# A transformer block with segment memory: the feed-forward part moved into the planned order, and work of the attention and opening stages placed on other engines

## The chip, the cores and the metric

The kernel runs on one core of one Trainium2 chip. A core has five engines that run side by side, each with its own queue in a fixed order: TensorE (PE in the profile) multiplies matrices, VectorE (DVE), ScalarE (ACT) and GpSimd (POOL) work on elements, SyncE (SP) issues DMAs. PSUM is the memory into which PE writes, in eight banks of 128 x 512 fp32; SBUF holds everything else on the chip. The metric is the time of one execution on the device in microseconds, lower is better. The time is the median of several runs.

## The reference, cut to what matters

```python
mod = (silu(c) @ w_mod)                  # six vectors of 512: sa, ca, ga, sb, cb, gb
h = layernorm(x) * (1 + ca) + sa         # x: 2048 x 512
q, k, v = h @ wq, h @ wk, h @ wv         # 32 heads of 16; 4 segments of 512 tokens
for s in range(4):                       # M, z: each head's memory, zero at first
    p = softmax(q_s k_s^T / 4 + causal mask)
    a_mem = phi(q_s) M / (phi(q_s) z + 1e-6)       # phi(t) = t + 1 if t > 0 else exp(t)
    o_s = g * a_mem + (1 - g) * p v_s              # g = sigmoid(beta), one per head
    M, z = M + phi(k_s)^T v_s, z + sum phi(k_s)
x = x + ga * (o @ wo)
h = layernorm(x) * (1 + cb) + sb
x = x + gb * (relu(h @ w1 + b1)**2 @ w2 + b2)      # 512 -> 1792 -> 512
```

All tensors are fp32.

## The kernel before, in words

**Precision.** A projection's two operands are each split into a high part, rounded to fp32r by a cast on ACT, and a low part, the rest, by a subtraction (`tensor_tensor`). Each product is three matmuls: high by high, high by low, low by high.

**Order.** The opening and the attention are written as nodes with `op(engine, duration, function, priority, after, get, put)`. `Plan.run` (L136) plays them through on a model with estimated durations: each engine takes the ready node of the lowest priority whose buffers are free, PE with some reluctance (`STAY`, `BATCH`, `PATIENCE`) to change between its three ways of tiling the array: R (row tiles), C (column tiles), F (full). `PL.emit()` then writes the instructions of PE, DVE, ACT and POOL in that order, which is fixed; waits keep it correct. SP's order comes from the framework. `POOLS` says how many buffers there are: eight PSUM banks, of which groups #A, #B, #V, #D may hold 4, 3, 1, 3 at a time, and SBUF buffers by name. The constants `K_...` are due times, in half units of attention.

**Opening.** DMAs bring x of the first segment, two parts of w_mod, then wq, wk, wv. `consts` loads c and beta on ACT's queue. `mod_cols` makes the shift and scale (`modc`). `ln1` normalises four tiles of 128 tokens, `ln_transposed` (L430) turns each on PE, applies scale and shift (two pieces of 128 columns on ACT, two on DVE, into one of two `oraw` buffers) and splits it into HT. `split_w` (L458) splits a weight in four row pieces: casts on ACT, subtractions on DVE and POOL in turn. Fourteen matmuls on the identity (L319) run ahead. `clear` fills rows of ST with zeros.

**Attention.** A unit u is 8 heads of one segment, 16 units in all; each has two half units (quads) of 4 heads. `qk` projects, copies high and low parts (L541, L543) and DMAs them into ST; from the second segment on, and for keys up to the third, it makes phi by exp and relu on ACT and `min(e, 1) + relu` on DVE (L552). `a_quad` (L603) computes the scores once for their row maxima: five groups of matmuls (L610), two on row tile 3 (`3i`), two on tiles 0 and 2 (`20i`), and, last, tile 1 of both pairs (`1`); each result is added to the mask `msk` and reduced by one custom DVE instruction (L615) and a read of its accumulator. The maxima are transposed (L658), negated and placed by DMA in ST as an extra row. `b_quad` (L731) computes the scores again (L739) with the maximum subtracted, takes exp on ACT (L754), zeroes the causal half of diagonal blocks on POOL (L743) and multiplies by V (L796). `mem` (L671) reads and updates the memory; `norm` (L833) divides; the gate's factors are `gt` = g and `omg` = 1 - g. `wo_tile` (L886) multiplies three segments by wo and adds x while attention still runs, `ln2(0)` normalises the first segment again.

**Feed-forward part.** It is not in the plan. After `PL.emit()` the attention's SBUF and PSUM pools are closed (L1018) and new ones opened: a bank for transposes, three (`pd2`) for the first matmuls, four (`pf`) for the outputs. `late_wo` does the last segment's wo tiles, then a loop (L1116) takes four strips of 512 tokens with 14 slices of 128 hidden columns each. `ffn1` is 12 matmuls (L1081 to L1083), relu and square on ACT, r*r and the low part on DVE (L1088, L1089); `ffn2` follows two slices later, 3 matmuls for each of four token tiles (L1101 to L1103). In the first strip the loop also loads and splits W1 and W2 (`load_w1`, `load_w2`, through the four `xr` buffers): cast on ACT, subtraction on POOL (L1050, L1057), for W2 a product with gb on DVE first (L1055). `ln2_tile` normalises the next strip's tiles; `x + gab` (L1099) runs on POOL.

Of the kernel before, what the change touches and what calls it, by code (L numbers as in the profile page):

```python
# [34 lines left out]
BATCH = {"R": 0.41, "C": 1.28, "F": 0.4}  # L35
K_A = (0.18, 1.18)
K_B = (1.6, 2.6)
K_F = 3.12
K_L2 = 0.42
K_LN = (-2.56, -1.76)  # L40
K_M = 3.73
K_MEM = (1.06, 0.9, 1.5)
K_P = (-2.0, -0.7, 0.8)
K_PV = (2.2, 2.5, 2.8)
K_QK = (0.54, 1.94)
K_QK0 = (1.0, 1.8)
K_ST = -3.39
K_T = -0.08
K_V = (-0.55, 1.44)
K_WO = -4.87  # L50
K_X = -5.5
PATIENCE = 0.66
STAY = {"R": 0.6, "C": 0, "F": 0.3}
# [6 lines left out]
class Plan:  # L60
# [3 lines left out]
    LAT = {"PE": 0.25, "ACT": 0.17, "DVE": 0.13, "POOL": 0.15, "SP": 0.0, "NIL": 0.0}  # L64
# [139 lines left out]
def block_kernel(ctx, tc, x, wq, wk, wv, wo, beta, w1, b1, w2, b2, c, wmod, out):  # L204
# [27 lines left out]
    gt = const.tile([P, H], F32, name="gt")  # L232
# [37 lines left out]
    for v in VT:  # L270
# [3 lines left out]
    POOLS = {"bank": 8, "#A": 4, "#B": 3, "#V": 1, "#D": 3, "xr": 4, "P": 3, "oraw": 2, "sg": 1, "e": 1, "phi0": 2,  # L274
             "phi1": 2, "pk": 1, "am": 3, "on": 2, "mx": 2, "mt": 1, "oT": 2, "mv": 2}
# [4 lines left out]
    def bank(key):  # L280
        if key not in TL:
# [4 lines left out]
              "pk": [P, 512], "am": [P, 4, NB, DH], "on": [P, 4, NB, DH], "mx": [P, 16], "mt": [16, P], "mv": [P, 4, 2],  # L286
# [54 lines left out]

    MODT = {}

    def mod_parts(m, pr, big=False, after=()):
# [24 lines left out]
        n = pe("C", 0.9, mm, pr + 0.02, after=[n_cs] + loads, get=[("#A" if big else "#D", b)], put=keys)  # L369
# [11 lines left out]
    def mod_cols(m, slot, plus, pr, big=False, after=()):  # L381
# [6 lines left out]
        n = pe("F", 0.9, mm, pr + 0.04, after=[MODT[m]], get=[("#A" if big else "#D", b)], put=[t])  # L388
# [28 lines left out]
    def ln_affine(eng, f, q, sc, bi):  # L417
        for k in (0, 1) if eng == "a" else (2, 3):
            src, dk = q[:, k * P:(k + 1) * P], f[:, k * P:(k + 1) * P]
            if eng == "a":  # L420
                nc.scalar.activation(dk, src, AF.Identity, scale=modc[:, sc, k:k + 1], bias=modc[:, bi, k:k + 1])
            else:
                nc.vector.tensor_scalar(dk, src, modc[:, sc, k:k + 1], modc[:, bi, k:k + 1], op0=ALU.mult, op1=ALU.add)

    def ln_split(dst, t, f):
        fv = f.rearrange("p (k n) -> p k n", k=KD)
        hi, lo = dst[:, 0, :, t * P:(t + 1) * P], dst[:, 1, :, t * P:(t + 1) * P]
        return (lambda: nc.scalar.copy(hi, fv)), (lambda: nc.vector.tensor_tensor(lo, fv, hi.bitcast(F32), op=ALU.subtract))  # L428

    def ln_transposed(s, t, src, dst, pool, sc, bi, pr, after, put, wait=()):  # L430
# [3 lines left out]
        n = pe("F", 0.44, lambda: ln_turn(bank(b), src()), pr, after=after, get=[("#D", b)], put=put)  # L434
        a1 = op("ACT", 0.68, lambda: ln_affine("a", buf(pool, f), bank(b), sc, bi), pr + 0.01, after=[n, *MODC[sc]],
                get=[(pool, f)], put=[b])
        a2 = op("DVE", 0.52, lambda: ln_affine("v", buf(pool, f), bank(b), sc, bi), pr + 0.01, after=[a1], put=[b])
        h = act(512, lambda: ln_split(dst(), t, TL[f])[0](), pr + 0.02, sbuf=True, after=[a1, a2, *wait], put=[f])
        l = dve(512, lambda: ln_split(dst(), t, TL[f])[1](), pr + 0.03, fast=True, after=[h], put=[f])
# [596 lines left out]
    def t2_tile():  # L1036
        return raw("t2")
# [117 lines left out]
```

## Time and profile before

| what | value |
|---|---|
| median of 3 runs | 883.96 us (883.91 to 886.72) |
| the profiled execution | 885.69 us |
| its span, first to last instruction | 884.0 us |
| mean granted PE clock | 0.977 |
| matmuls / DVE instructions | 4864 / 1770 |

The page also has the span in 40 equal slices, each digit a busy share in tenths:

```profile
PE   6899999999989999999989998898899999999998
DVE  5889877789897788878997977865634324333223
ACT  3536754556754657465563552444323322322221
POOL 3202210123211231222211113755401000000000
PEclk9799999999998999999998999999899999999999
```

A slice is 22.1 us. The opening is the first slice and the beginning of the second, attention runs to the 24th, the rest is the feed-forward part, with POOL's weight splits in slices 25 to 29. The profile models the ends of pipelined matmuls, so PE's busy share says little of how fast it works; the idle time before an instruction, the granted clock (PEclk) and what released a wait say more.

### The profile page before, as it was taken

The page shows a single profiled execution, that of the slowest core. Times are in us where ns is not written, and L with a number is a line of the kernel's source. Part 1 is how long each engine was busy: PE and PEld are TensorE (multiplying, and loading weights), DVE is VectorE, ACT ScalarE, POOL GpSimd, SP SyncE. Part 2 cuts the span into 40 slices and gives each one's busy share as a digit, 9 for nine tenths or more (in the row PEclk, how much of TensorE's full clock was granted, in tenths as well). Part 3 has the DMA queues.
Part 4 walks back from the last instruction along what each step waited for, and adds up shares of the span by engine and source line. Part 5 has one row for each costly group of instructions (what it writes and reads, how often), then busy time and mean ns, then how long its engine had stood idle before and what let it go on. Part 6 is the DMA issues. An engine that isn't in the chain of part 4 may idle for free.

```text
span 884.0 us, 14322 instructions
## 1 busy us (share of the span) xinstructions
PE 833.0 (94%) x4864; PEld 590.8 (67%) x4864; DVE 596.9 (68%) x1770; ACT 405.5 (46%) x819; POOL 175.2 (20%) x211
## 2 busy tenths in 40 slices
PE   6899999999989999999989998898899999999998
PEld 4655555655556655666546667686688888888886
DVE  5889877789897788878997977865634324333223
ACT  3536754556754657465563552444323322322221
POOL 3202210123211231222211113755401000000000
PEclk9799999999998999999998999999899999999999
DMA  8723454123430334123342223322010001001001
GB/s 285 187 66 75 114 185 120 25 74 90 127 73 13 85 86 103 47 70 85 73 114 91 76 100 113 96 72 83 25 49 1 0 1 48 1 0 48 1 1 47
DMA packets 50378, 65.19 MB, mean 74 GB/s; under 512 B 8449, under 2 KB 22529, under 8 KB 50306
## 3 DMA queue, kind: packets, MB, share of 16 engines
q1 hardware_dynamic: 49490, 64.13, 25.6%
q8 instruction: 39, 0.64, 0.3%
q10 hardware_dynamic: 816, 0.15, 0.1%
q14 instruction: 33, 0.27, 0.1%
HBM read 29.91 MB, written 7.34 MB: 42 GB/s over the span
## 4 chain that ended last, share of the span: by engine, by line
PE 59%; DVE 27%; issue 5%; DMA 3%; POOL 3%; ACT 1%; SPq 1%; DVEq 0%; POOLq 0%; ACTq 0%
DVE ba L615 12%; PE pf L1103 5%; PE pf L1101 5%; PE pf L1102 5%; PE pd L1082 4%; PE pd L1081 4%; PE pd L1083 4%; PE bpv L796 4%; PE bpb L739 4%; PE ba L610 3%; PE bqk L529 2%; DVE mx L615 2%; PE bqk L530 2%; PE bqk L531 2%; PE bv L581 2%
## 5 line engine op out<-in xcount | busy, mean ns | idle before, releaser
L615 DVE CUSTOM_DVE_ANT_0 ba<-ba,msk 128x384 f32<-128x384 f32 (+3 forms) x512 | 244.3, 512 | 33.9 <-PE ba L610 26.9
L754 ACT ACTIVATE pt<-bpb 128x512 f32<-128x512 f32 x320 | 175.7, 606 | 56.4 <-PE bpb L739 51.3
L743 POOL TENSOR_SCALAR_AFFINE_SELECT pt<-pt 128x512 f32<-128x512 f32 x128 | 83.0, 661 | 339.3 <-ACT pt L754 279.7
L1085 ACT ACTIVATE r<-pd,b1c 128x512 f32<-128x512 f32 x56 | 38.6, 690 | 189.7 <-PE pd L1083 168.5
L1088 DVE TENSOR_TENSOR r<-r 128x512 f32<-128x512 f32 x56 | 43.6, 779 | 120.1 <-ACT rr L1087 120.1
L1103 PE MATMUL pf<-W,rr 128*128 128x512 f32 x224 | 89.0, 400 | 8.4 <-DVE rr L1089 8.3
L739 PE MATMUL bpb<-ST 64*128 64x256 f32 (+2 forms) x512 | 90.7, 387 | 6.1 <-DVE mx L615 4.7
L1101 PE MATMUL pf<-W,rr 128*128 128x512 f32 x224 | 89.7, 400 | 0.0
L739 PEld LDWEIGHTS bpb<-ST 64*128 64x128 f32 x512 | 45.5, 186 | 65.8 <-issue 24.6
L1102 PE MATMUL pf<-W,rr 128*128 128x512 f32 x224 | 88.8, 397 | 0.0
L610 PE MATMUL ba<-ST 63*128 63x256 f32 (+2 forms) x512 | 79.6, 348 | 6.0 <-DVE mx L615 2.8
L796 PE MATMUL bpv<-pt,VT 128*32 128x512 f32 (+3 forms) x1024 | 83.8, 443 | 0.1
L615 DVE DVE_READ_ACCUMULATOR2_ANT mx<- 128x1 f32 x512 | 72.7, 142 | 0.0
L610 PEld LDWEIGHTS ba<-ST 63*128 63x128 f32 x512 | 52.2, 188 | 25.6 <-DVE mx L615 10.0
L529 PE MATMUL bqk<-HT,WQK 128*128 128x512 f32 x128 | 58.3, 456 | 9.2 <-ACT HT L428 7.0
L1103 PEld LDWEIGHTS pf<-W,rr 128*128 128x128 f32 x224 | 42.8, 192 | 19.6 <-DVE rr L1089 10.5
L530 PE MATMUL bqk<-HT,WQK 128*128 128x512 f32 x128 | 51.2, 400 | 0.6 <-DVE HT L428 0.6
L531 PE MATMUL bqk<-HT,WQK 128*128 128x512 f32 x128 | 51.2, 400 | 0.0
L1102 PEld LDWEIGHTS pf<-W,rr 128*128 128x128 f32 x224 | 42.8, 191 | 8.9
L1101 PEld LDWEIGHTS pf<-W,rr 128*128 128x128 f32 x224 | 42.8, 191 | 8.9
L1089 DVE TENSOR_TENSOR rr<-r,rr 128x512 fp32r<-128x512 f32 x56 | 43.6, 779 | 4.1
L1083 PE MATMUL pd<-H2a,W 128*128 128x512 f32 x112 | 44.6, 399 | 1.6 <-POOL W L1050 1.6
(168 smaller groups left out, 1472.1 us busy)
## 6 DMA issues: line engine op xcount, KB each, us to landing
ST<-sg SPq DMA_DIRECT2D x192, 128.0 KB
w<-in_B_w SPq DMA_DIRECT2D x28, 256.0 KB
xt<-in_A_x SPq DMA_DIRECT2D x20, 256.0 KB
wm<-in_w_mod SPq DMA_DIRECT2D x16, 256.0 KB
o_dram<-on SPq DMA_DIRECT2D x12, 256.0 KB
ot<-o_dram SPq DMA_DIRECT2D x12, 256.0 KB
xw<-in_A_x SPq DMA_DIRECT2D x12, 256.0 KB
out<-X SPq DMA_DIRECT2D x12, 256.0 KB
```

The source lines that it names most:

```text
L529: nc.tensor.matmul(p, wh, HT[:, 0, k], start=(k == 0), stop=False)
L530: nc.tensor.matmul(p, wh, HT[:, 1, k], start=False, stop=False)
L610: nc.tensor.matmul(dst[:, c0:c0 + n], ST[b:b + 63, 0, sl, qt * P:(qt + 1) * P], ST[b:b + 63, 1, sl, :n], start=True, stop=True)
L615: nc.vector.tensor_tensor_reduce(i, i, msk[:, 512 - n:], scale=1.0, scalar=-3e38, op0=ALU.add, op1=ALU.max, accum_out=o)
L739: nc.tensor.matmul(dst, ST[b:b + 64, 1, sl, kb * P:(kb + 1) * P], ST[b:b + 64, 0, sl, q0:512], start=True, stop=True)
L743: nc.gpsimd.affine_select(out=ap, in_=ap, pattern=[[0, ap.shape[1]], [1, P]], compare_op=ALU.is_ge, fill=0.0, base=0, channel_multiplier=-1)
L754: ns = [act(512, lambda j=j: nc.scalar.activation(buf("P", pt)[:, i + j], bank(keys[j]), AF.Exp, scale=0.25), pr[slot] + 0.01 + 0.001 * j, ...
L796: nc.tensor.matmul(bank(o)[32 * hq:32 * hq + 32, q0:q0 + src.shape[1]], v[:, a:a + 32], src, start=start, stop=stop, tile_position=(0, 32 ...
L1083: nc.tensor.matmul(p, wl, h2[:, 0, k], start=False, stop=(k == KD - 1))
L1101: nc.tensor.matmul(p, rh, W2[:, f, 0], start=(f == 0), stop=False)
L1102: nc.tensor.matmul(p, rh, W2[:, f, 1], start=False, stop=False)
L1103: LAST["f"] = nc.tensor.matmul(p, rl, W2[:, f, 0], start=False, stop=(f == NF - 1))
```

## The change: what it does

1. **Feed-forward part in the plan.** `late_wo`, `load_w1`, `load_w2`, `ffn1`, `ffn2` and the later `ln2` become nodes of the same plan, with due times from `z = e + K_FF` in steps of 0.4 per slice. The PSUM pool stays open to the end; a new group #F may hold four banks for the outputs, and the first matmuls and the norm's transposes share #D (three). A node `N_FFN` after all earlier nodes closes the attention's SBUF pools and opens W1, W2 and the rest. Weights are loaded through two buffers of their own (`wr`). Their low parts are made on DVE, as is `x + gab`: POOL has nothing to do in this part.
2. **Opening.** `split_w` works on column pieces of 128: the first piece of each weight is split by ACT and DVE, the other three by ACT and POOL, and for wq and wk these come later (`K_W`). wq is loaded into X1L, wv ahead of the ST clears. The four `lnf` tiles of the first segment get four buffers and its transposes #A banks. beta's load moves from ACT's queue to SP's, with a later due time, and the gates wait for it. In place of the fourteen matmuls at the start, sixty on the identity are nodes of the lowest priority (50.0), which PE takes when nothing else is ready in the plan.
3. **Score maxima.** Group `1` comes first: its two banks are copied to SBUF by ACT (`ac`), masked by one `affine_select` on POOL and reduced by one `tensor_reduce` on DVE, in place of four custom reductions.
4. **phi and the first norm.** The minimum and the sum of phi move from DVE (one instruction) to POOL (two). For segments 1 to 3 all four affine pieces are on ACT and the low part on POOL.
5. **Small.** `gate` needs one instruction less (`gt` is gone; the added epsilon and a factor `ge` = 1/g are one step), one buffer fewer of `phi0` and of `on`, the estimated durations of many nodes and all due times are new.

The diff, cut to its core (the due times and durations are left out):

```diff
+N_WARM = 60
...
+    wk_ = ("warm",)
+    for i in range(N_WARM):
+        pe("F", 0.22, lambda: nc.tensor.matmul(bank(wk_)[:, :P], ident, ident, start=True, stop=True), 50.0,
+           get=[("bank", wk_)] if i == 0 else (), put=[wk_], after=[n_w0] if i else ())
...
-        for k in range(KD):
-            hi, lo = W3(w, k, 0, 0, D), W3(w, k, 1, 0, D)
...
+        for cc in range(4):
+            c0 = slice(cc * P, (cc + 1) * P)
+            hi, lo = full[:, :, 0, c0], full[:, :, 1, c0]
+            p = pr + 0.01 * cc + (late if cc else 0.0)
...
+            pool = cc > 0
...
-                PHN[u, w] = op("DVE", 0.48, lambda e=e, f=f: nc.vector.scalar_tensor_tensor(TL[f], TL[e], 1.0, TL[f], op0=ALU.min,
...
+                m_ = op("POOL", 0.7, lambda e=e: nc.gpsimd.tensor_scalar(TL[e], TL[e], 1.0, None, op0=ALU.min), p2 + 0.002, after=[x1_])
+                PHN[u, w] = op("POOL", 1.4, lambda e=e, f=f: nc.gpsimd.tensor_tensor(TL[f], TL[f], TL[e], op=ALU.add), p2 + 0.003,
+                               after=[m_, x2_], put=[e])
...
+        cp = [act(512, lambda j=j: nc.scalar.copy(buf("ac", ac)[:, j], bank(keys[j])), pr[0] + 0.01 + 0.001 * j, after=[first],
+                  put=[keys[j]]) for j in (0, 1)]
...
+        def hide():
+            v = acv()[:, :, P:]
+            nc.gpsimd.affine_select(out=v, in_=v, pattern=[[0, 4], [-1, P]], compare_op=ALU.is_ge, fill=NEG, base=0,
+                                    channel_multiplier=1)
+        n = op("POOL", 0.6, hide, pr[0] + 0.02, after=cp)
+        reds.append(op("DVE", 1.15, lambda: nc.vector.tensor_reduce(
+            buf("mx", mx).rearrange("p (a t) -> p a t", t=4)[:, :, 1], acv(), axis=AX.X, op=ALU.max), pr[0] + 0.3,
+            after=[n], put=[ac]))
...
-        group("1", 4, 0.24, m1, 0.69, lambda m, j, p: [red(m[:, j, i, 1:2], p[:, 256 * i:256 * i + 256]) for i in (0, 1)],
-              [2 * qd, 2 * qd + 1])
...
+    def load_w1(f, pr):
+        k = ("wr1", f)
+        wv_ = lambda: wraw(k).rearrange("p (k n) -> p k n", k=KD)
+        n = sp(lambda: nc.sync.dma_start(wv_(), w1[:, f * P:(f + 1) * P].rearrange("(k p) n -> p k n", p=P)), pr - 0.2,
+               1 << 18, after=[N_FFN], get=[("wr", k)])
+        n = act(512, lambda: nc.scalar.copy(FF["W1"][:, f, 0], wv_()), pr, sbuf=True, after=[n], put=[k])
+        W1N[f] = dve(512, lambda: nc.vector.tensor_tensor(FF["W1"][:, f, 1], wv_(), FF["W1"][:, f, 0].bitcast(F32), op=ALU.subtract),
+                     pr + 0.01, after=[n], put=[k])
...
-                nc.gpsimd.tensor_tensor(x1(g), x1(g), b2g, op=ALU.add)
...
+            F2[s, t, "x"] = dve(512, lambda: nc.vector.tensor_tensor(x1(g), x1(g), gab, op=ALU.add), pr, after=[n_b2, X1L2[g]])
```

More of the change, by code (lines that the diff above doesn't have):

```diff
@@ L31 @@
 VROW = NB * VA
[L35 to L41, printed above, removed]
-K_MEM = (1.06, 0.9, 1.5)
[L43 to L53, printed above, removed]
+N_WARM = 60
+BATCH = {"R": 0, "C": 1.28, "F": 0.28}
+K_A = (0.08, 1.18)
+K_B = (1.46, 2.6)
+K_F = 3.4
+K_FF = 3.98
+K_L2 = 0.37
+K_LN = (-2.92, -1.85)
+K_M = 4.37
+K_MEM = (1.06, 0.9, 1.5)
+K_P = (-2.51, -1.02, 0.41)
+K_PV = (2.36, 2.5, 2.96)
+K_QK = (0.54, 1.66)
+K_QK0 = (0.49, 1.1)
+K_ST = -3.82
+K_T = -0.14
+K_V = (-0.58, 1.0)
+K_W = 2.0
+K_WO = -4.55
+K_X = -5.53
+PATIENCE = 1.22
+STAY = {"R": 0.53, "C": 0, "F": 0.38}
 class Node:
@@ L60 @@
 class Plan:
-    LAT = {"PE": 0.25, "ACT": 0.17, "DVE": 0.13, "POOL": 0.15, "SP": 0.0, "NIL": 0.0}
+    LAT = {"PE": 0.25, "ACT": 0.17, "DVE": 0.2, "POOL": 0.15, "SP": 0.0, "NIL": 0.0}
     LDW = {"R": 0.11, "C": 0.03, "F": 0.11}
@@ L699, in mem @@
                 MRD[u].append(n)
[L700 removed]
+                outs_.append(op("DVE", 0.87, lambda h2=h2, b=b: gate(h2, b), pr[h2] + 0.01, after=[n, n_gate], put=[b]))
             AMN[u] = outs_
@@ L840, in norm @@
                                     den[:, :, :, None].to_broadcast([P, 4, 4, DH]), op=ALU.mult)
-        k = ONN[u, qd] = op("DVE", 0.65, norm, p_fin + 0.02, after=[k], put=[b])
+        k = ONN[u, qd] = op("DVE", 0.84, norm, p_fin + 0.02, after=[k, n_gate], put=[b])
         if qd == 1:
@@ new lines, in block_kernel @@
+    for f in range(NF):
+        load_w1(f, z + ST2 * (f - 1.5))
+        load_w2(f, z + ST2 * (f + 0.5))
+    for t in range(4):
+        wo_tile(4 * NS - 4 + t, z - 2 + 0.3 * t)
+    kb = ("b2b",)
+    n = sp(lambda: nc.sync.dma_start(buf("xr", kb), bass.AP(tensor=b2.tensor, offset=b2.offset, ap=[[0, P], [1, D]])), z + 0.2, 1 << 18,
+           get=[("xr", kb)], after=[X1N[4 * NS - 1]])
+    n_b2 = dve(512, lambda: nc.vector.tensor_tensor(gab, TL[kb], FF["gbb"], op=ALU.mult), z + 0.4, after=[n, n_gbb], put=[kb])
@@ new lines, in block_kernel @@
+    LAG = 2
+    RR = {}
+    for s in range(NS):
+        if s:
+            ln2(s, [z + ST2 * ((s - 1) * NF + 4 + 2 * t) for t in range(4)], [F1[s - 2, NF - 1]] if s > 1 else WOL)
+        for f in range(NF):
+            RR[s, f] = ffn1(s, f, z + ST2 * (s * NF + f))
+        for f in range(NF):
+            for t in range(4):
+                last = s == NS - 1 and f >= NF - 2
+                ffn2(s, f, t, z + ST2 * (s * NF + (NF - 1 if last else f) + LAG) + (0.02 * t + 0.001 * f if last else 0.001 * t), RR[s, f])
@@ L1052, in load_w2 @@
-    def load_w2(f):
-        w = raw("w2")
-        nc.sync.dma_start(w, w2[f * P:(f + 1) * P, :])
-        nc.vector.tensor_tensor(w, w, gbb, op=ALU.mult)
-        nc.scalar.copy(W2[:, f, 0], w)
-        nc.gpsimd.tensor_tensor(W2[:, f, 1], w, W2[:, f, 0].bitcast(F32), op=ALU.subtract)
-    LT["op"] = lambda: sb2.tile([P, 2, 512], F32R, name="oT", tag="rr", bufs=3)
-    b2g = gab
-    def late_wo():
-        bank = iter(range(4))
-        hold = []
-        for t in range(4):
-            hold.append(wo_last(4 * NS - 4 + t, lambda: pf_tile(next(bank)), pd2))
-            if t > 0:
-                hold.pop(0)()
-        hold.pop(0)()
-        b2b = raw("b2b")
-        nc.sync.dma_start(b2b, bass.AP(tensor=b2.tensor, offset=b2.offset, ap=[[0, P], [1, D]]))
-        nc.vector.tensor_tensor(b2g, b2b, gbb, op=ALU.mult)
```

385 lines of the change are left out of this document (173 added, 212 removed).

## Prediction

> **What bounds the kernel now.** I read the page's head and chain first, for the share of each engine.
>
> ```profile
> span 884.0 us, 14322 instructions
> PE 833.0 (94%) x4864; PEld 590.8 (67%) x4864; DVE 596.9 (68%) x1770; ACT 405.5 (46%) x819; POOL 175.2 (20%) x211
> PE 59%; DVE 27%; issue 5%; DMA 3%; POOL 3%; ACT 1%; SPq 1%; DVEq 0%; POOLq 0%; ACTq 0%
> ```
>
> TensorE (PE) is busy nearly always, yet VectorE (DVE) holds 27% of the chain that ended last. An average over stages hides why, so I cut the span where the program changes stage: opening, attention, the hand-over to the feed-forward part, its first strip (while weights are still being split), the rest, the tail. The columns after the stretch's length are busy us of PE, PEld, DVE, ACT, POOL, then the granted clock.
>
> ```profile
> 18.00:25.50 7.50, 0.49 (x5) 0.25 (x4) 7.01 (x15) 7.28 (x17) 3.66 (x3) 0.72 0.96 240
> 25.50:31.70 6.20, 5.63 (x13) 4.12 (x14) 6.20 (x5) 3.06 (x6) 4.95 (x4) 0.51 0.95 280
> 46.00:536.00 490.00, 465.07 (x3264) 294.34 (x3263) 411.23 (x1466) 280.03 (x594) 97.50 (x144) 0.98 0.32 86
> 536.00:548.00 12.00, 11.96 (x54) 9.80 (x52) 8.64 (x20) 3.39 (x6) 2.65 (x3) 0.86 0.35 104
> 548.00:640.00 92.00, 81.81 (x336) 63.74 (x335) 62.34 (x77) 37.73 (x66) 53.35 (x36) 0.94 0.24 73
> 640.00:880.00 240.00, 240.00 (x1069) 197.37 (x1067) 82.43 (x131) 65.21 (x108) 7.74 (x6) 1.00 0.04 16
> ```
>
> Four things are to be seen. Just before 25.5 us PE stands still for 7.0 us, and then it works 6.2 us at half clock. In attention PE is idle 490 − 465.1 = 24.9 us with DVE busy 84% of the time (411/490). From 548 to 640 PE is idle 10.2 us and the clock dips. From 640 to 880 PE is never idle at full clock: 240 us that no change of order can shorten. Idle and half-clock time outside that last stretch is what the change can win.
>
> **Opening.** The wait that ends last there, and the work in front of it on DVE:
>
> ```profile
> PE bqk L529 <- ACT HT L428: 7.0, 1, 7.0
> 18.47 1.34 DVE L471 TENSOR_TENSOR WQK<-w,WQK 128x512 fp32r<-128x512 f32 x1 [0.27 <-ACT WQK L469]
> 22.78 0.68 DVE L471 TENSOR_TENSOR WQK<-w,WQK 128x512 fp32r<-128x512 f32 x1
> 24.85 1.95 DVE L428 TENSOR_TENSOR HT<-lnf,HT 128x512 fp32r<-128x512 f32 x2
> ```
>
> The first projection waits for the normalised input HT, which ends at 24.85 + 1.95 = 26.8 us. Between its pieces DVE does weight splits (1.34 and 0.68 us: 2.0). The change splits only the first 128 columns of wq and wk before that, gives the four tiles four buffers instead of two, so that the second pair no longer waits for the first, and takes silu ahead of the statistics. The other three quarters of each split go to POOL, behind wv's; they are due when the second unit is projected, a unit's projections and the whole value projection later, which hides them. DMA issues move too: beta goes from ACT's queue to SP's, behind the weights, and wv passes the ST clears on SP; gates and clears are used from the first attention units on (46 us in my cut), so their later start is covered. I take 3 us of the 7.0: DVE's 2.0 of splits plus about 1 of buffer wait. Sixty filler matmuls fill PE's hole; half clock lost 6.2 × 0.49 = 3.0 us, of which I take 2, since a hole may remain where the planner's clock and the chip's differ. Together −5 (bounds: −1 if the loads end last anyway, −9 if the whole idle and clock loss goes but 1).
>
> [...]
>
> **Attention.** Rows for what leaves DVE, then for what ACT and POOL gain, all of 46 to 536 us:
>
> ```profile
> L615 DVE CUSTOM_DVE_ANT_0 ba<-ba,msk 128x256 f32<-128x256 f32 x128 | 54.6, 446 | 2.2
> L615 DVE CUSTOM_DVE_ANT_0 ba<-ba,msk 128x384 f32<-128x384 f32 (+3 forms) x512 | 244.3, 512 | 33.9 <-PE ba L610 26.9
> L411 DVE TENSOR_SCALAR xt<-xt,mv 128x512 f32<-128x512 f32 x8 | 4.0, 554 | 0.0
> L552 DVE SCALAR_TENSOR_TENSOR phi<-e,phi 128x512 f32<-128x512 f32 x23 | 17.1, 744 | 0.0
> L423 DVE TENSOR_SCALAR lnf<-blnq,modc 128x128 f32<-128x128 f32 x32 | 11.6, 404 | 0.1
> L428 DVE TENSOR_TENSOR HT<-lnf,HT 128x512 fp32r<-128x512 f32 x12 | 8.2, 687 | 5.2 <-ACT HT L428 5.2
> L689 DVE TENSOR_TENSOR den<-den,gt 128x16 f32<-128x16 f32 x24 | 4.2, 176 | 0.8
> L818 ACT COPY oraw<-bpv 128x512 f32<-128x512 f32 x32 | 19.1, 597 | 12.7 <-PE bpv L796 12.6
> L421 ACT ACTIVATE lnf<-blnq,modc 128x128 f32<-128x128 f32 x32 | 13.3, 479 | 1.9 <-PE blnq L415 0.7 <-DVE HT L428 0.6 <-PE bmodc L387 0.6
> L743 POOL TENSOR_SCALAR_AFFINE_SELECT pt<-pt 128x512 f32<-128x512 f32 x128 | 83.0, 661 | 339.3 <-ACT pt L754 279.7 <-DVE mx L615 31.8 <-ACT mt L660 22.0
> L845 POOL TENSOR_TENSOR on<-on,am 128x512 f32<-128x512 f32 x8 | 10.3, 1282 | 14.5 <-DVE on L839 14.5
> ```
>
> DVE loses the 128 maxima of width 256 (54.6 us) and gets 32 plain maxima over 1,024 elements. No row has such a reduction; the nearest one-input pass over 512 takes 554 ns, so 32 × 2 × 0.554 = 35 (bounds 20 and 45): −20. It loses phi (−17), 24 of the 32 affine pieces (24 × 0.404 = −10; the other 8 are the second norm's), the 12 low parts (−8) and one small gate step (−4). That is 59 us, 14% of 411: DVE falls to 352.
>
> ACT gains 64 bank copies (64 × 0.597 = 38) and 24 affine pieces (24 × 0.479 = 11): 280 becomes 329. POOL gains 32 maskings (32 × 0.661 = 21), 24 minima (bounded by 0.661, 16), 24 additions and 12 low parts (36 × 1.28 = 46): 97 becomes 180. In a stretch of 465 us that is DVE 76%, ACT 71%, POOL 39%: PE's 465 then stands clearly above every other engine.
>
> The masked maximum now has a chain of waits: both copies on ACT, POOL's mask, DVE. Exps queue behind the copies on ACT, and the score transpose waits for the maximum. It is issued first of five groups, so the other groups' maxima on DVE, (244.3 − 54.6)/32 = 5.9 us per half unit, cover its two copies and mask (2 × 0.60 + 0.66 = 1.9); uncovered, it would cost that per half unit. Phi now comes from POOL after 0.66 + 1.28 = 1.9 instead of 0.74 us; its first reader's due time (2u + 0.9 in K_MEM) lies over one half unit, 490/32 = 15 us, behind the projection's (2u − 2 + 1.66 at the latest in K_QK), which hides that. Only one buffer of phi0 and of on is left: the next unit's write of either, on ACT or DVE, now waits for this unit's readers or its store. The norms wait for the gates as well, which are long done.
>
> Two estimates of the gain: DVE's place on the chain is 27% of 884 = 239 us, and 14% of it is 33; PE's idle plus half-clock time is 24.9 + 0.02 × 490 = 35. I take 25, since some waits are on ACT's exps and on DMA, which stay. Bounds: 0 (the waits move to ACT or POOL) and 50 (stops hidden inside pipelined matmuls, which the page counts as busy, go as well).
>
> **Hand-over and feed-forward.** The weight splits on POOL, and the same DVE line while POOL works (548 to 640) and after (640 to 884):
>
> ```profile
> L1057 POOL TENSOR_TENSOR W<-w,W 128x512 fp32r<-128x512 f32 x13 | 20.2, 1564 | 19.5 <-ACT W L1056 19.5
> L1099 POOL TENSOR_TENSOR X<-X,gab 128x512 f32<-128x512 f32 x10 | 14.5, 1465 | 10.1 <-DVE gab L1072 5.6 <-DVE xh L411 4.5
> L1089 DVE TENSOR_TENSOR rr<-r,rr 128x512 fp32r<-128x512 f32 x13 | 13.9, 1069 | 0.7
> L1089 DVE TENSOR_TENSOR rr<-r,rr 128x512 fp32r<-128x512 f32 x43 | 29.8, 692 | 3.4
> L428 DVE TENSOR_TENSOR WVO<-t,WVO 128x512 fp32r<-128x512 f32 x4 | 7.1, 1785 | 0.0
> L428 DVE TENSOR_TENSOR WVO<-t,WVO 128x512 fp32r<-128x512 f32 x4 | 2.7, 686 | 0.0
> PE pf L1103 <- DVE rr L1089: 8.3, 4, 3.7
> 553.83 1.28 POOL L1050 TENSOR_TENSOR W<-w,W 128x512 fp32r<-128x512 f32 x1
> 553.93 1.20 DVE L404 TENSOR_SCALAR lny<-lnv 128x4 int32<-128x4 int32 x1
> 593.27 0.34 SPq L1054 DMA_DIRECT2D w<-in_B_w  x1
> 595.85 0.69 DVE L1055 TENSOR_TENSOR w<-w,gbb 128x512 f32<-128x512 f32 x1 [2.60 <-DMA w<-in_B_w]
> ```
>
> A step over 4 columns took 1.20 us while one POOL operation lasted 1.28, and full-size DVE steps take 1.07 to 1.79 instead of 0.69: DVE stands still while POOL reads. PE's waits in the strip are for exactly that DVE step. The change leaves POOL nothing here. What can go is the idle 10.2 plus clock 0.06 × 92 = 5.5, plus 0.14 × 12 = 1.7 in the hand-over: 17.4 us.
>
> Some comes back. Per slice of hidden columns DVE does five steps of 0.69, 3.5 us, beside PE's 24 matmuls at 240/1069 us, 5.4; with the second norm's tiles and the added X + gab (one 0.69 per tile) it can still hold that. The norm's transposes now share three banks with the first matmuls instead of having one of their own. The loads have two buffers of their own instead of four shared ones: a pair is ready every 0.34 + 2.24 to landing + 0.69 + 0.60 (a copy like L818) + 0.69 = 4.6 us, 0.8 under the period, and 0.3 us of queueing before each of three steps uses that up. I therefore take 13 (bounds 5 and 19).
>
> **Sum.** The profiled execution took 885.69 us, 1.7 around its span. 885.7 − 5 − 25 − 13 = 842.7; the median shown is 883.96, 1.7 below that execution, so 841.0.
>
> **Rivals.** *POOL stops DVE in attention* (chance 0.17). The rows above show what a POOL operation does to DVE. The change puts some 60 such operations into attention; if each stopped DVE for 1.0 us (1.20 for L404's 4 columns, against 0.18 for L689's 16), the 59 us of relief would be gone and only 5 + 13 remain: 866. Against it: most of DVE's attention work reads PSUM and one SBUF operand, and the maxima keep their pace now beside 128 selects. [...]
>
> *Attention gains double* (0.17): DVE's 239 us on the chain are mostly queueing that vanishes once it is under PE. −50 instead of −25: 816. Against it: PE shows only 25 us of plain idleness.
>
> *ACT turns into the wait* (0.07, slower): 64 copies stand in one queue with the 320 exps that PE's banks wait for. If a half unit loses 2 us to that, 32 × 2 = 64 against 43 gained: 905. It decides from 43/32 = 1.35 us per half unit. For it, 71% load in a fixed order; against it, ACT's longest waits now are for PE.
>
> *Nothing* (0.04): the new order has as many waits as the old: 884.
>
> **Numbers.** The forecast has 0.55 and its own range 826 to 856 from the bounds above. The overall range 815 to 868 takes in the POOL rival and about half of the double gain; it leaves out 0.08 below and 0.11 above. About 0.3% is what a measurement of this kernel can tell from no change. Faster 0.55 + 0.17 + 0.17 = 0.89, same 0.04, slower 0.07.
>
> **What would show it.** Opening: HT done near 23 us and full clock from the first projection. Attention: DVE near 76% busy, PE idle under 10 us, fewer than three half-clock dips. Feed-forward: the DVE steps at 0.69 from the first strip, PE waits for them gone. Wrong would be: PE idle in attention as before with ACT or POOL named as releaser, POOL-long DVE steps there, or weight loads as the wait in the first strip.

## The result, and the profile after

The kernel after takes 842.62 us (median of 4 runs, 841.85 to 843.69) where the kernel before took 884.2 beside it: a ratio of 0.9525, 95% interval [0.9503, 0.9547]. The forecast was 841.0 in a range of 815 to 868. Its profiled execution took 843.69 us, 42.0 less than the one of before. First the page's head and its chain, the same three lines as for before:

```profile
span 842.0 us, 14276 instructions
PE 819.5 (97%) x4956; PEld 592.8 (70%) x4956; DVE 549.6 (65%) x1503; ACT 441.0 (52%) x907; POOL 211.5 (25%) x262
PE 85%; DVE 7%; ACT 4%; DMA 2%; issue 1%; SPq 0%; DVEq 0%; ACTq 0%
```

DVE's place on the chain fell from 27% to 7%, PE's rose from 59% to 85%. To see where the 42 us came from I cut both spans at the same four events: the first matmul of the first projection, the first score matmul, the end of the last output transpose (L842 in the kernel after), and the first matmul of the feed-forward part. The traces give these times:

| kernel | first projection | first score | last output transpose | first feed-forward matmul | span |
|---|---|---|---|---|---|
| before | 25.5 | 45.7 | 533.4 | 550.1 | 884.0 |
| after | 27.0 | 48.9 | 501.2 | 516.3 | 842.0 |

By differences: the opening up to the first score is 3.1 us **longer**, attention is 487.7 − 452.3 = 35.4 shorter, the hand-over 16.7 − 15.1 = 1.6 shorter, the rest 333.9 − 325.7 = 8.2 shorter. Now the windows of before that these cuts need (length; busy us of PE, PEld, DVE, ACT, POOL; granted clock; the last two columns, the DMA share and GB/s, are not used here), and then those of after:

```profile
45.70:533.40 487.70, 464.97 (x3261) 294.17 (x3260) 408.70 (x1457) 280.18 (x594) 97.50 (x144) 0.98 0.32 86
533.40:550.10 16.70, 14.47 (x65) 11.98 (x65) 13.08 (x32) 4.01 (x7) 4.75 (x4) 0.90 0.35 110
```

```profile
2.00:13.70 11.70, 11.70 (x88) 11.60 (x88) 8.12 (x28) 0.77 (x2) 3.92 (x9) 1.00 0.97 339
23.00:27.00 4.00, 0.23 (x3) 0.03 (x1) 3.57 (x5) 3.91 (x10) 1.18 (x1) 0.89 1.05 196
27.00:37.50 10.50, 10.47 (x33) 8.16 (x34) 5.09 (x10) 6.54 (x13) 6.99 (x6) 0.72 0.48 160
48.90:501.20 452.30, 444.01 (x3248) 286.90 (x3247) 359.35 (x1144) 311.39 (x678) 192.11 (x234) 1.00 0.34 91
501.20:516.30 15.10, 10.61 (x49) 8.85 (x49) 12.42 (x35) 5.44 (x12) 0.00 (x0) 0.77 0.39 125
...
516.00:606.00 90.00, 90.00 (x399) 73.22 (x398) 67.48 (x121) 39.85 (x68) 0.00 (x0) 1.00 0.28 85
606.00:838.00 232.00, 232.00 (x1019) 187.95 (x1018) 83.01 (x130) 65.54 (x106) 0.00 (x0) 1.00 0.04 13
```

Row by row: PE is busy from the first microseconds, with fillers; it then idles 4.00 − 0.23 = 3.8 us just ahead of the first projection, which runs at a clock of 0.72 after all. In attention idle fell from 22.7 to 8.3 us and the clock rose from 0.98 to 1.00. The hand-over is worse filled than before: 4.5 us idle instead of 2.2, clock 0.77 instead of 0.90. From 516 on PE is never idle, at full clock, in the first strip too.

The opening in single instructions (start, duration, instruction, count, and in brackets the idle time before it). The first modulation product of before, and then the same place and the first projection of after:

```profile
9.19 0.62 PE L367 MATMUL bmod<-wmod,cs 128*32 128x512 f32 x1 [1.09 <-DVE cs L327]
```

```profile
13.40 0.39 PE L334 MATMUL bwarm<-ident 128*128 128x128 f32 x2
13.72 1.06 PE L365 MATMUL bmod<-wmod,cs 128*32 128x512 f32 x8
27.03 0.79 PE L536 MATMUL bqk<-HT,WQK 128*128 128x512 f32 x1 [3.81 <-ACT HT L426]
```

Fillers stand directly ahead of the product, which starts 4.5 us later than before without a wait of its own.

Last, the groups of attention on DVE and POOL that the forecast had priced (busy us, mean ns, idle before and its releasers), the feed-forward's DVE step in the first strip, and one small DVE step at a time when POOL is idle:

```profile
L661 DVE TENSOR_REDUCE mx<-ac 128x4 f32<-128x1024 f32 x32 | 39.0, 1218 | 7.3 <-POOL ac L658 6.1
L402 DVE TENSOR_SCALAR lny<-lnv 128x4 int32<-128x4 int32 x4 | 2.6, 647 | 0.1
L559 POOL TENSOR_SCALAR e<-e 128x512 f32<-128x512 f32 x23 | 34.2, 1486 | 28.4 <-ACT e L555 28.2
L560 POOL TENSOR_TENSOR phi<-phi,e 128x512 f32<-128x512 f32 x23 | 29.4, 1277 | 1.4
...
L1082 DVE TENSOR_TENSOR rr<-r,rr 128x512 fp32r<-128x512 f32 x15 | 10.4, 693 | 1.1
...
506.98 0.17 DVE L402 TENSOR_SCALAR lny<-lnv 128x4 int32<-128x4 int32 x1
```

### The profile page after: what moved, and what is told of

It reads as the page before. It is cut to its first block, busy times and chain, and to the rows that moved or that the text cites. A ratio compares the mean times of both kernels' runs of the same rounds, so it can differ in the third digit from the quotient of the medians.

```text
span 842.0 us, 14276 instructions
## 1 busy us (share of the span) xinstructions
PE 819.5 (97%) x4956; PEld 592.8 (70%) x4956; DVE 549.6 (65%) x1503; ACT 441.0 (52%) x907; POOL 211.5 (25%) x262
## 4 chain that ended last, share of the span: by engine, by line
PE 85%; DVE 7%; ACT 4%; DMA 2%; issue 1%; SPq 0%; DVEq 0%; ACTq 0%
PE bpv L816 8%; PE bpb L759 7%; PE bh L1065 6%; PE bh L1064 6%; PE bh L1066 6%; PE bpf L1092 6%; PE bpf L1094 6%; PE bpf L1093 6%; PE ba L617 5%; PE bqk L536 4%; PE bqk L537 3%; PE bqk L538 3%; PE bwop L900 2%; PE bv L588 2%; DVE ba L622 2%; PE bwop L902 2%
## 5 line engine op out<-in xcount | busy, mean ns | idle before, releaser
L622 DVE CUSTOM_DVE_ANT_0 ba<-ba,msk 128x512 f32<-128x512 f32 (+2 forms) x384 | 191.8, 533 | 38.2 <-PE ba L617 33.3
L1074 ACT ACTIVATE r<-bh,b1c 128x512 f32<-128x512 f32 x56 | 38.5, 688 | 180.4 <-PE bh L1066 163.3
L1081 DVE TENSOR_TENSOR r<-r 128x512 f32<-128x512 f32 x56 | 38.7, 691 | 126.8 <-ACT rr L1078 126.7
L759 PE MATMUL bpb<-ST 64*128 64x256 f32 (+2 forms) x512 | 87.1, 387 | 1.7 <-DVE X1L L859 1.2
L1092 PE MATMUL bpf<-W,rr 128*128 128x512 f32 x224 | 88.1, 393 | 0.0
L1094 PE MATMUL bpf<-W,rr 128*128 128x512 f32 x224 | 88.0, 393 | 0.0
L1093 PE MATMUL bpf<-W,rr 128*128 128x512 f32 x224 | 88.0, 393 | 0.0
L617 PE MATMUL ba<-ST 63*128 63x256 f32 (+2 forms) x512 | 72.3, 336 | 1.4 <-ACT lnf L419 0.5
L816 PEld LDWEIGHTS bpv<-pt,VT 128*32 128x32 f32 x1024 | 26.2, 109 | 41.5 <-issue 35.0
L622 DVE DVE_READ_ACCUMULATOR2_ANT mx<- 128x1 f32 x384 | 54.4, 142 | 0.0
L1092 PEld LDWEIGHTS bpf<-W,rr 128*128 128x128 f32 x224 | 42.1, 188 | 10.0
L1093 PEld LDWEIGHTS bpf<-W,rr 128*128 128x128 f32 x224 | 42.0, 188 | 9.8
L1094 PEld LDWEIGHTS bpf<-W,rr 128*128 128x128 f32 x224 | 42.0, 188 | 9.8
L1064 PE MATMUL bh<-H2a,W 128*128 128x512 f32 x112 | 45.1, 403 | 0.0
```

The source lines that it names most:

```text
L617: nc.tensor.matmul(dst[:, c0:c0 + n], ST[b:b + 63, 0, sl, qt * P:(qt + 1) * P], ST[b:b + 63, 1, sl, :n], start=True, stop=True)
L622: nc.vector.tensor_tensor_reduce(i, i, msk[:, 512 - n:], scale=1.0, scalar=-3e38, op0=ALU.add, op1=ALU.max, accum_out=o)
L759: nc.tensor.matmul(dst, ST[b:b + 64, 1, sl, kb * P:(kb + 1) * P], ST[b:b + 64, 0, sl, q0:512], start=True, stop=True)
L816: nc.tensor.matmul(bank(o)[32 * hq:32 * hq + 32, q0:q0 + src.shape[1]], v[:, a:a + 32], src, start=start, stop=stop, tile_position=(0, 32 ...
L1064: nc.tensor.matmul(p, wh, h2[:, 0, k], start=(k == 0), stop=False)
L1092: nc.tensor.matmul(p, rh, FF["W2"][:, f, 0], start=(f == 0), stop=False)
```

## The experiments

The theory after reading the traces: attention gained by the relief of DVE; the feed-forward part by POOL's silence; the opening gained nothing because the fillers stand in PE's fixed order ahead of work that was ready. Rivals: the new due times made the gain in attention; N_FFN or the buffers made the hole in the hand-over; the clock, not the fillers' place, holds the opening. All kernels below are edits of the kernel after. Each median is set against runs of before on the same chip, so kernels that ran on different chips are compared by ratio; stage times are from the profiled executions, cut as above.

One caution belongs ahead of all. The plan is played through anew for each kernel, so an edit can change the order of all engines far from its place. Eight kernels have (nearly) the same instructions in attention: after, and the seven below that edit only the opening, the hand-over or the first strip. Four of them (after, the one with 24 fillers, the one with the splits on POOL, the one with the norm behind N_FFN) also have the very same recorded order there on PE, DVE, ACT and POOL; from first score to last output transpose they take 452.3, 450.3, 452.2 and 452.6 us, 2.3 us of spread in one order. The other four have other orders and take 451.4 (other only in its last tenth), 453.5, 459.4 and 461.8 us. So where an edit changes the order, a difference in attention below some 10 us is not safely due to the work that it moved; a difference at the place of the edit is.

**Where attention's gain comes from: four kernels that give work back to DVE.** All reliefs undone (maxima by custom reductions, phi in one DVE step, the norm's affine and low parts on DVE):

```diff
-        cp = [act(512, lambda j=j: nc.scalar.copy(buf("ac", ac)[:, j], bank(keys[j])), ...)]
-        n = op("POOL", 0.6, hide, pr[0] + 0.02, after=cp)
-        reds.append(op("DVE", 1.15, lambda: nc.vector.tensor_reduce(...)))
+        def halves(j):
+            for i in (0, 1):
+                red(mxv()[:, j, i, 1:2], bank(keys[j])[:, 256 * i:256 * i + 256])
...
-                m_ = op("POOL", 0.7, ... nc.gpsimd.tensor_scalar(TL[e], TL[e], 1.0, None, op0=ALU.min) ...)
-                PHN[u, w] = op("POOL", 1.4, ... nc.gpsimd.tensor_tensor(TL[f], TL[f], TL[e], op=ALU.add) ...)
+                PHN[u, w] = dve(512, ... nc.vector.scalar_tensor_tensor(TL[f], TL[e], 1.0, TL[f], op0=ALU.min, op1=ALU.add) ...)
...
-                                    [("xt", g)], HUSE[s - 1], "POOL" if s else "DVE", ...)
+                                    [("xt", g)], HUSE[s - 1], "DVE", ...)
```

> The changed kernel with its three reliefs of VectorE undone: the tile-1 maxima by custom reductions from PSUM, phi's minimum and sum in one VectorE step, and half of the first norm's affine pieces and all its low parts on VectorE. Due times, the planned feed-forward part, the opening and the fillers stay. If attention gained because VectorE was relieved (my theory), VectorE goes back to about 415 us of work in attention and the gain of 33 us there is mostly lost: 870 us (864 to 878), and VectorE is again the releaser of PE's waits. If the new due times and durations brought it, the time stays within 5 us of 842.6. Half and half would be about 856.

Measured: 859.67 us, ratio 0.9735 [0.9715, 0.9754], between the two theories and nearest to half and half. The other three kernels undo one block of this diff each: the maxima alone, phi alone, the norm alone.

> Only the tile-1 maxima go back to VectorE (four custom reductions of width 256 in place of two copies on ACT, a mask on GpSimd and one reduction). VectorE gets about 20 us more, ACT 36 less, GpSimd 21 less. Relief theory: a third of the loss, +8 to +12, 852 us. Order theory: 843. If ACT's copies stood in the way of the exps, it would be faster than 842.6 instead.

> Only phi's minimum and sum go back to VectorE, one step of 0.66 to 0.74 us in place of 1.49 and 1.28 us on GpSimd. VectorE gets 17 us more, GpSimd 64 less. Relief theory: +6 to +11, 851 us. Order theory: 843. If GpSimd's phi operations stop VectorE as they did in the feed-forward part before, the step costs nothing net or is faster: 838 to 843.

> Only the first norm of segments 1 to 3 goes back: two of four affine pieces and the low part on VectorE. VectorE gets 18 us more, ACT 11 less, GpSimd 15 less. Relief theory: +6 to +11, 851 us. Order theory: 843.

Measured: 847.3, ratio 0.9602 [0.9586, 0.9618]; 856.82, ratio 0.9706 [0.9691, 0.9722]; 848.96, ratio 0.9622 [0.9606, 0.9638]. The windows of attention, in the order all, maxima, phi, norm:

```profile
49.50:516.80 467.30, 451.38 (x3248) 289.00 (x3247) 400.85 (x1427) 275.56 (x590) 94.87 (x144) 1.00 0.34 88
```

```profile
48.60:505.70 457.10, 449.55 (x3248) 287.74 (x3247) 375.28 (x1368) 283.18 (x614) 173.07 (x202) 0.99 0.34 90
```

```profile
48.60:512.20 463.60, 452.73 (x3248) 289.62 (x3247) 371.84 (x1167) 310.59 (x678) 130.48 (x188) 0.99 0.34 89
```

```profile
49.20:504.80 455.60, 444.62 (x3248) 286.90 (x3247) 372.62 (x1180) 305.30 (x654) 178.58 (x222) 1.00 0.34 91
```

What follows: with DVE loaded with 401 us again, nearly as in before (409), attention takes 467.3, not 487.7. The reliefs are worth 15.0 of the 35.4 us. I had expected VectorE to be the releaser of PE's waits again; it is so only in part: of PE's 15.9 us of idle time DVE is named for 6.4 and ACT for 5.7. Each single undoing makes the kernel slower in total, its interval clear of that of after: the norm at the lower end of the relief theory, the maxima between the two theories, phi above both. In attention itself only phi, 11.3 us, lies outside the range named above, and narrowly (463.6 against 461.8); the maxima (4.8) and the norm (3.3) don't, and the three sum to 19.4, not 15.0. The price is not in proportion to DVE's time: phi gives DVE 12.5 us of work, the maxima 15.9. Why phi is worth the most was not tested further.

The third kernel also answers the POOL rival. POOL's work in attention falls there from 192 to 130 us, and the new reduction stays as it is:

```profile
L661 DVE TENSOR_REDUCE mx<-ac 128x4 f32<-128x1024 f32 x32 | 38.9, 1216 | 7.1 <-POOL ac L658 7.1
```

It takes 1216 ns there and 1218 in the kernel after. In the latter five of the 32 even ran beside a POOL addition over two SBUF tiles for their whole length, and took 1221 to 1224 ns; one of them:

```profile
287.45 1.22 DVE L661 TENSOR_REDUCE mx<-ac 128x4 f32<-128x1024 f32 x1
287.40 1.29 POOL L865 TENSOR_TENSOR on<-on,am 128x512 f32<-128x512 f32 x1
```

POOL does not stop this reduction: 1221 to 1224 ns beside it, 1218 in the mean of all 32.

**What the due times are worth.** All of after, but the due times of the attention and the planner's constants are those of before (K_F, which sets the output step of a unit, the second norm's, the feed-forward's and the opening's stay, and so do the estimated durations):

```diff
-BATCH = {"R": 0, "C": 1.28, "F": 0.28}
-K_LN = (-2.92, -1.85)
-K_QK = (0.54, 1.66)
-PATIENCE = 1.22
+BATCH = {"R": 0.41, "C": 1.28, "F": 0.4}
+K_LN = (-2.56, -1.76)
+K_QK = (0.54, 1.94)
+PATIENCE = 0.66
...
-    LAT = {"PE": 0.25, "ACT": 0.17, "DVE": 0.2, ...}
+    LAT = {"PE": 0.25, "ACT": 0.17, "DVE": 0.13, ...}
```

(and K_A, K_B, K_M, K_P, K_PV, K_QK0, K_ST, K_T, K_V, K_WO, K_X, STAY likewise)

> Kernel after with every relief of DVE kept, but the due times of the attention part and the planner's constants (batch, patience, stay, DVE's latency) those of the kernel before; the opening's and the feed-forward's stay. The reliefs together account for 15 of the 33 us that attention gained. Theory (the other 18 come from the order, which was fitted anew to the lighter DVE): attention takes 14 to 18 us longer, 857 to 860, with PE idle 15 us or more there. Rival (the 18 come from the durations that the planner now knows better and from the smaller edits, and the due times are worth little): within 4 us of after, 842 to 846.

Measured: 868.85 us, ratio 0.9828 [0.9806, 0.985]. Its windows of attention and hand-over, and PE's longest wait in them (total, times, longest):

```profile
49.00:511.80 462.80, 450.80 (x3209) 285.19 (x3209) 350.25 (x1129) 308.28 (x669) 192.64 (x234) 0.98 0.33 89
511.80:540.20 28.40, 21.08 (x88) 16.80 (x88) 19.69 (x49) 9.44 (x20) 0.00 (x0) 0.76 0.23 69
```

```profile
PE blnq L413 <- DVE xh L409: 7.3, 4, 3.0
```

The total is above both expectations. Attention itself takes 10.5 us longer, less than the theory's 14 to 18, with 12.0 us idle and the clock at 0.98; but some 40 matmuls that fill attention in the kernel after (28 of `wo_tile`, 12 turns of the second norm) slid into the hand-over, which takes 28.4 us instead of 15.1. From first score to first feed-forward matmul the row is: before 504.4, after 467.4, reliefs undone 482.3, due times undone 491.2. So of 37.0 us gained there, 23.8 are lost when the due times alone are undone, and 14.9 when the reliefs alone are. The 23.8 is the price of old due times in a relieved kernel, mixed with some new ones, not safely what the new ones add by themselves; no kernel has both undone, so how the two work together is not shown, and that they add up to about the whole (38.7) may be chance.

**Opening: fewer fillers, then fillers at another place.** First only 24 instead of 60:

```diff
-N_WARM = 60
+N_WARM = 24
```

> 24 filler matmuls in place of 60. In the changed kernel the fillers stand in PE's queue until 13.6 us, and the first modulation product starts only then. If they set the start of the chain to the first projection, the product starts near 10.5 us when its weights have landed and the whole kernel is 3 us faster: 839.5. If the loads set it, nothing moves: 842.6. In both cases the first projection still runs at half clock, since PE idles before it.

Measured: 839.16 us, ratio 0.9508 [0.9482, 0.9535], as forecast; the interval still meets that of after, so the gain is read at its place below. Then the 24, and 80 more which are ready once the first of the two modulation columns is there:

```diff
+    wl_ = ("warmlate",)
+    for i in range(80):
+        pe("F", 0.11, lambda: nc.tensor.matmul(bank(wl_)[:, :P], ident, ident, start=True, stop=True), 50.0,
+           get=[("bank", wl_)] if i == 0 else (), put=[wl_], after=[n_w1] if i else [n_ca])
...
```

> 24 fillers at the start and 80 more that become ready once the first modulation columns are there, so that they fill PE's hole before the first projection. If the clock falls only because PE idles there, the first projection runs at full clock and 3 us go on top of the 3 us of the run with 24 fillers: 836.5. If late fillers stand in front of needed work as the early ones did, it is not faster than with 24 fillers.

Measured: 846.16 us, ratio 0.9588 [0.9565, 0.9611]. Then 30 of these, with the planner's duration at 0.22, ready once both columns (`n_ca`, `n_sa`) are there:

> Kernel after with 24 fillers at the start and 30 late ones, ready once both modulation columns are there, so that they fill only the hole ahead of the first projection (about 17.3 to 23.3 us in the run with 24 fillers, where PE idled 6.6 us and the first projection then ran at half clock). Theory (the fillers cost 4 us because they stand ahead of the modulation product, and help only if they end when the normalised input is there): first projection at about 23.4 us as with 24 fillers, but at full clock to the first value projection (7.3 us instead of 10.4); that is 3 us under the run with 24 fillers and 6 under after: about 836. Rival (the clock, or the transfers behind it, take the gain back): as with 24 fillers or worse, 838 to 840.

Measured: 843.53 us, ratio 0.9545 [0.9527, 0.9564]. The windows ahead of the first projection, from it to the first value projection, and of attention; 24 fillers, 80 late ones, 30 late ones:

```profile
16.70:23.30 6.60, 0.05 (x1) 0.00 (x0) 5.58 (x13) 6.43 (x15) 3.71 (x3) 0.66 1.03 301
23.30:33.80 10.50, 10.46 (x34) 8.15 (x35) 5.06 (x10) 6.43 (x13) 7.59 (x6) 0.72 0.74 168
...
45.10:495.40 450.30, 442.44 (x3248) 286.57 (x3247) 359.24 (x1144) 311.21 (x678) 192.10 (x234) 1.00 0.35 92
```

```profile
17.30:31.10 13.80, 13.80 (x125) 13.80 (x125) 8.25 (x18) 10.14 (x22) 9.25 (x8) 1.00 0.96 251
31.10:38.80 7.70, 7.70 (x37) 6.38 (x36) 1.75 (x4) 2.17 (x4) 1.50 (x2) 1.00 0.12 9
```

```profile
16.50:23.20 6.70, 6.70 (x60) 6.58 (x59) 5.74 (x13) 6.54 (x16) 3.74 (x3) 1.00 1.02 301
23.20:31.40 8.20, 7.97 (x34) 6.30 (x34) 6.14 (x10) 6.37 (x14) 7.06 (x6) 1.00 0.91 215
...
42.70:502.20 459.50, 450.09 (x3250) 289.95 (x3249) 359.55 (x1144) 311.63 (x678) 192.65 (x234) 0.99 0.34 90
```

With 24 fillers the first projection starts at 23.3 instead of 27.0: those 3.7 us were the fillers in front of the product. The hole is then 6.6 us long and the clock falls (0.66, then 0.72). Eighty late fillers keep the clock up (1.00) but run to 31.1 us, 7 us past the moment at which HT's last high part was there (24.0); 22 of their 160 matmuls even ran inside attention. Thirty fill the hole (58 of 60 matmuls stand in it): no idle, full clock (1.00), first score at 42.7 instead of 48.9. So the opening had 6.1 us to give, and the theory of the fillers' place is right. The last row tells why the total shows none of it: attention, with nearly the same instructions, takes 459.5 us instead of 452.3 in the order that was drawn for it. All of the loss arises early: a quarter of the 1,024 matmuls with V have started 141.2 us after the first score instead of 134.3, and from there the two kernels keep step. In that stretch this kernel has a dip of the clock, 3.4 us at 98.0 us, that after lacks (attention's mean clock 0.99 against 1.00), which costs up to 1.7 us. PE's idle time in all of attention rose by 1.1 only (9.4 against 8.3). The rest lies in matmuls that the page counts as busy, and which of their waits did it stays open.

**First strip: the splits back on POOL.**

```diff
-        W1N[f] = dve(512, lambda: nc.vector.tensor_tensor(FF["W1"]...
+        W1N[f] = op("POOL", 1.45, lambda: nc.gpsimd.tensor_tensor(FF["W1"]...
...
```

(W2 and `x + gab` likewise)

> The feed-forward part stays in the plan, but the low parts of W1 and W2 and the sum X + gab go back to GpSimd. If the gain of about 16 us in the first strip came from keeping GpSimd off VectorE's inputs, VectorE's steps there are 1.1 to 1.8 us again, PE idles about 10 us and dips to half clock: 855 us (850 to 860). If the planned order alone brought it, it stays within 3 us of 842.6.

Measured: 851.71 us, ratio 0.9656 [0.9626, 0.9687]. The first strip's window, and the DVE step that PE waits for:

```profile
516.20:606.20 90.00, 85.08 (x367) 66.59 (x366) 56.30 (x80) 38.49 (x67) 50.03 (x35) 1.00 0.24 74
```

```profile
L1082 DVE TENSOR_TENSOR rr<-r,rr 128x512 fp32r<-128x512 f32 x13 | 14.7, 1130 | 0.9
```

PE's idle time is back, 4.9 us in 90 (half of what I expected, and without the dip of the clock: 1.00), and the step takes 1130 ns instead of 693. From the last output transpose to the last matmul this kernel takes 344.6 us, after 336.9, before 346.9: 7.7 of the 10.0 us hang on POOL's silence, and this stage's order ahead of the strip did not change (15.1 in both).

**Hand-over: first the place of the norm in the plan,** behind N_FFN instead of ahead of it:

```diff
-    ln2(0, [e + K_L2 + 0.3 * t for t in range(4)])
...
+    ln2(0, [e + K_L2 + 0.3 * t for t in range(4)])
```

> The second norm of the first segment is entered into the plan behind the node that opens the feed-forward part, so that the last segment's wo tiles and the weight loads no longer wait in the plan for that norm's end. In the changed kernel PE idles 4.5 us of the 15 between attention and feed-forward part and falls to half clock, about 8 us lost in all. If that dependence is the cause, PE has matmuls to fill the hole: 837 us (834 to 840). If the norm's own chain through VectorE, PE and ACT sets the start of the first strip, it stays at 842.6.

Measured: 844.94 us, ratio 0.9568 [0.9538, 0.9598]. The hand-over's window is longer, with about the same idle time, 4.4 us:

```profile
502.00:520.90 18.90, 14.46 (x57) 11.41 (x57) 14.11 (x38) 5.81 (x12) 0.00 (x0) 0.73 0.43 125
```

So N_FFN isn't the cause. **Then the norm's buffers:** its affine pieces go to the two buffers of phi1, which the last segment doesn't use, instead of sharing four `xr` buffers with the applied tiles.

```diff
-                             get=[("xr", xh), ("xr", ("lnf", CB, s, t))])
-            H2N[s] += ln_transposed(..., "xr", CB, SB, pr[t], [a], [xh], wait)
+                             get=[("xr", xh)] + ([("xr", ("lnf", CB, s, t))] if s else []))
+            H2N[s] += ln_transposed(..., "xr" if s else "phi1", CB, SB, pr[t], [a], [xh], wait)
```

> Kernel after where the affine pieces of the first strip's four norm tiles go to the two buffers of phi1, which no unit of the last segment uses, instead of taking two of the four xr buffers with each tile. Theory (the hand-over's hole is the four tiles standing in one row for those buffers): the 4.5 us of PE idle and 3.4 us of lost clock between the last output transpose and the first feed-forward matmuls mostly go, about -5: 837.5; PE's waits for the applied tile xh vanish. Rival (the row of steps on ACT, DVE and PE sets the hole, whatever the buffers): unchanged within 1.5 us, 841 to 843.5. Slower is possible if the x tiles of the last segment's output projection, which are now loaded behind the first weights, come late: +2.

Measured: 840.79 us, ratio 0.9511 [0.9493, 0.953]. PE's waits from 495 to 520 us, after and this kernel, and this kernel's window:

```profile
PE blnq L413 <- DVE xh L409: 5.3, 3, 2.7
```

```profile
PE bwot L925 <- DVE X1L L865: 2.1, 1, 2.1
PE bwop L902 <- DVE oT L933: 0.2, 1, 0.2
```

```profile
500.20:514.30 14.10, 11.80 (x52) 9.30 (x51) 11.74 (x31) 4.05 (x8) 0.00 (x0) 0.88 0.47 139
```

The wait for xh is gone; the next one, for the attention's last output (X1L), is 2.1 us. The stage from last output transpose to last matmul takes 333.1 us instead of 336.9. The buffers set 3.8 us of it, where I had expected 5 (eight kernels that leave this stage alone take 336.4 to 337.5): 2.3 us of idle time and a clock of 0.88 stay in the hand-over. In total the gain can't be told from nothing: the two intervals overlap.

**Both edits, the late fillers and the buffers.**

> Both edits of the two runs above in one kernel. They lie 450 us apart, so their gains should add: about 831 to 833 if both theories hold; 837 if one holds; 840 or more if neither does.

Measured: 840.4 us, ratio 0.9516 [0.9495, 0.9537].

```profile
42.70:504.50 461.80, 454.91 (x3260) 292.35 (x3260) 363.14 (x1153) 313.89 (x684) 192.67 (x234) 0.99 0.34 89
504.50:518.70 14.20, 11.76 (x53) 9.27 (x51) 11.87 (x32) 4.08 (x8) 0.00 (x0) 0.88 0.52 142
```

Both gains are there again at their places: first score at 42.7, and 333.3 us from last output transpose to last matmul. Attention takes 461.8 us, 9.5 more than in after, and eats most of both; it has the order of the kernel with 30 late fillers almost to its end, so that order was slow twice. The expected 831 to 833 was missed for that reason: I had added stage gains as if the stage between them stayed put. No kernel of this study is measurably faster than the kernel after.

## Why the prediction was right, and where it was not

The total, 841.0 against 842.62, is right in part by luck, by terms that err on both sides: forecast −5, −25, −13, measured +3.1, −35.4 and −1.6 − 8.2 = −9.8, which is the 42 us by which the span fell.

**Opening: the wrong sign.** The step that failed is "sixty filler matmuls fill PE's hole". I took a priority in the plan for a priority on the chip. PE's order is fixed in advance by the model's clock; the plan put most fillers in front of the modulation product, and there they ran on the chip, though the product could start at 9.05 us (with 24 fillers) instead of 13.72. The last ones ended near 23.2 us, the hole was still there behind them (3.8 us), and the clock fell all the same (0.72 over the 10.5 us from the first projection on). That alone explains 3.7 us, by the kernel with 24 fillers. "HT done near 23 us" and "full clock from the first projection" were the tests I had named; both failed, and both hold once 30 fillers stand in the hole. The longer way from first projection to first score (21.8 instead of 20.2 us) goes with one more projection group ahead of the first score (33 recorded projection matmuls instead of 24): work moved forward rather than added. In before and after each dip of the clock ahead of the end lasts 3.4, 6.8 or 10.2 us. With 30 fillers in the hole the clock is 1.00 from 2.0 us to the first score at 42.7, so there the whole clock term is won. What brings a dip the traces do not settle: the clock halved 2.9 us into the holes of before (at 21.35 us) and after (at 26.08 us), 2.1 us into that of the kernel with 24 fillers, and once without a long hole (last section). My 2 of 3.0 was too little for well placed fillers and too much for these.

**Attention: right direction, but two causes where I priced one.** DVE fell to 359 us of busy time (352 forecast), 79% of the stage; PE idle 8.3 us (under 10 forecast), one half-clock dip (3.4 us) instead of three (3.4, 6.8 and 6.8 us). Yet the relief of DVE, from which all of my 25 us came, was worth 15.0. I left out a term, the due times and planner's constants: undone alone they cost 10.5 in attention, 23.8 with the hand-over. I had read the diff's new constants as bookkeeping, and my two estimates, chain share times relief and idle plus clock, could not separate a lighter engine from a better order: both take the same idle time away.

**Single prices.** The reduction measured 39.0 us (35 forecast, bounds 20 and 45). POOL's minimum, bounded by 0.661, took 1.486: the nearest row was another kind of instruction. POOL had room for it, busy 42% of the time (192 us, 180 forecast). ACT rose to 311 (329 forecast).

**Rivals.** *POOL stops DVE*: falls. The 4-column step does lengthen, from 0.17 to a mean of 0.65 us, but there are few such steps, and phi back on DVE makes the kernel slower, not faster. *ACT as the wait*: falls; PE's waits for ACT in attention sum to 2.2 us. *Attention gains double* came part of the way, 35 instead of 50, and not by DVE's queueing alone. The waits for ACT (total, times, longest):

```profile
PE bpv L816 <- ACT pt L774: 0.9, 2, 0.6
PE ba L617 <- ACT lnf L419: 0.5, 1, 0.5
PE bfin L842 <- ACT oraw L838: 0.5, 2, 0.2
PE ba L617 <- ACT phi L557: 0.3, 1, 0.3
```

**Feed-forward: the mechanism as forecast, the size smaller.** The DVE step takes 0.69 us from the first strip, PE has no wait there, and with the splits back on POOL 7.7 us return. What I had not seen is the hand-over: I counted its lost clock as winnable, but it got worse, because each tile of the second norm needs two of four shared buffers and so the tiles wait for one another. That is 3.8 us, a little more than the difference between 13 and 9.8.

## What to carry to other kernels

A filler, or any work of low priority, in an order fixed in advance runs where the model put it; place it by a dependency on the event ahead of the hole, and make it as long as the hole. When a planner draws the order, price its constants as an edit of their own, and judge an upstream edit at its place in the trace as well as by the total: here nearly the same instructions took 450 to 453 us in one order and up to 462 in others, more than most single edits were worth. Compare the recorded orders first: where they agree, the total can be trusted further.

## What the runs showed that I had not expected

One filler node is two matmul instructions in the trace (30 nodes, 60 matmuls, 58 of them in the 6.7 us of the hole: 0.11 us each). POOL's `tensor_scalar` minimum over 128x512 takes 1.49 us, more than its `tensor_tensor` over two such tiles (1.28) and more than twice its `affine_select` (0.65). And with an idle time of 3.8 us ahead of the first projection after had half clock for 6.8 us (26.1 to 32.9), where the kernel with 24 fillers had 6.6 us of idle and 10.2 of half clock. The kernel with the norm's buffers, whose edit lies behind the opening, had only 3.4 us of half clock there (0.82 from 28.0 to 37.5 us); what sets the length was not shown. In after the clock also halved at 428.9 us, where PE had stood idle for only 1.3 us in the 3.4 us before:

```profile
425.40:428.85 3.45, 2.18 (x18) 1.48 (x20) 3.31 (x12) 2.50 (x5) 1.72 (x3) 1.00 0.81 223
428.85:432.30 3.45, 3.45 (x22) 1.67 (x21) 2.69 (x12) 2.00 (x5) 0.14 (x1) 0.51 0.65 211
```
